# Reading float32 tiles under a float32r name in the transposes of a fused attention and two feed-forward layers

## The chip, the cores and the metric

The program runs on one core of one Trainium2 chip. The metric is the device time of one execution in microseconds, the median of several runs. The profile is one execution of the same program, taken by the hardware profiler.

## The reference

The input is four batches of eight heads, 576 positions and 64 elements a head, all in float32. What is computed is an attention with a threshold, and behind it two feed-forward layers on the 2304 x 512 result:

```
scores = scale * q @ k.T
scores = where(scores >= max(scores) - tau, scores, -1e9)
attn   = exp(scores - max(scores)); attn /= sum(attn) + 1e-9
x = (attn @ v), heads side by side            # 2304 x 512
x = (s * relu(x @ w_in)**2 + b) @ w_out       # 512 -> 2048 -> 512
out = leaky(x @ w2_in) @ w2_out               # the same sizes, one slope for each of 2048 columns
```

## The kernel before

Work is added as tasks (`add`), each with an engine, a planned cost in microseconds, a rank, and the buffers that it reads and writes. `Plan.run` then plays these tasks through on planned costs and writes each engine's instruction order, so that the order of every queue follows from the planned costs as well as from the ranks. The chip afterwards runs each queue in that order.

Attention works on 16 pairs of heads, four pairs to a batch. For a pair, the natural rows of k, q and v are loaded (three `nat` tiles for all pairs, four `v32` tiles of their own for the first four pairs). TensorE (PE) turns k and q in `transpose` at L658 to L662: runs of four transposes of 128 x 128 each (two runs a pair) and one single transpose of the tails. Nine score tiles of 128 x 576 follow (L742). VectorE (DVE) takes the maximum (L752), ScalarE (ACT) the exponentials into one of six `e` tiles (L756), and DVE applies the threshold and sums (L758). `group` then turns five column blocks of the exponentials for each of four groups of a pair, at L874 to L881. Such a run is two transposes at L877 (`gi` is 0), or two at L877 and a third at L881 (`gi` is 1), so there are 160 runs of two and 160 runs of three. ACT, DVE and POOL split each turned block into a high and a low float32r part, and PE multiplies by v at L852. At the end `by_sums` spreads the reciprocals into `rb`, turns them at L811 (12 runs of four, 8 runs of two), and DVE multiplies `z` by them (L814). The result goes to the DRAM tensor `xs`.

All transposes read float32: the tile that is turned is the stationary operand of PE and the identity in `eyes` streams through. The other products outside the first four pairs are float32r with high and low parts (`mm3`, L480 to L482, three passes).

The first feed-forward layer is in two blocks of work. Block A (six blocks of 256 positions, ten of the sixteen slices of the hidden size) has rank `LATER`, so that PE takes it where no attention task is ready. It needs `xs` of its positions. Block B (the rest, 384 positions at a time) may start only when attention has given its memory back and its own rows have been loaded into `xr` (L493) and split into `xb` (L497, L498); ACT and DVE meanwhile turn the remaining weights into float32r halves in `wb` (the last step at L411). The second layer follows with a seven-product scheme.

Of the kernel before, what the change touches and what calls it, by code (L numbers as in the profile page):

```python
# [9 lines left out]
F32 = mybir.dt.float32  # L10
F32R = mybir.dt.float32r
# [6 lines left out]
P = 128  # L18
# [42 lines left out]
class Slots:  # L61
# [4 lines left out]
    def add(self, tiles):  # L66
        self.free.extend(tiles)
# [152 lines left out]
def tile_kernel(ctx: ExitStack, tc: tile.TileContext, q, k, v, tau, w1i, w1o, s_in, b_in, w2i, w2o, alpha, out):  # L220
    nc = tc.nc
    B, H, S, D = q.shape
# [6 lines left out]
    NQ = S // P  # L229
    TL = S - NQ * P  # L230
    NK = NQ + 1
# [9 lines left out]
    add = plan.add  # L241


    def pe(n, k=1):
        return k * max(0.109, n / 2400.0 + 0.0025)

    def pe_r(n, k=1):

        return k * (n / 2400.0 + (0.0135 if n < 512 else 0.0205))
# [17 lines left out]
    const = ctx.enter_context(tc.tile_pool(name="const", bufs=1))  # L267
# [6 lines left out]
    def tiles(pool, n, name, shape, dt=F32):  # L274
        return [pool.tile(shape, dt, name=f"{name}{i}") for i in range(n)]

    eyes = const.tile([P, P + P // 2], F32, name="eyes")
    ident = eyes[:, :P]
    swap = eyes[:, P // 2:]
    tau_b = const.tile([P, 1], F32, name="tau_b")  # L280
    s_b = const.tile([P, 1], F32, name="s_b")
    b_b = const.tile([P, 1], F32, name="b_b")
# [36 lines left out]
    rb_s, yb_s = Slots(), Slots()  # L319

    xt = mp.tile([P, NC * 2 * TA], F32R, name="xt")
    gt = mp.tile([P, NGA * 4 * TA], F32R, name="gt")
# [234 lines left out]

    def attention(ap):
        STEP = 10.0
        nat_s = Slots(tiles(ap, 3, "nat", [P, NK, 2, D]))  # L560
        vt_s, gh_s, gl_s, gr_s = Slots(), Slots(), Slots(), Slots()

        q_s = Slots(tiles(ap, 1, "q", [P, 2, NQ * P], F32R))
        k_s = Slots(tiles(ap, 1, "k", [P, S], F32R))
        hq = ap.tile([P, 2, NK * P], F32R, name="hq")
        hq_s, hk_s = Slots([hq]), Slots(tiles(ap, 1, "hk", [P, 2, S], F32R))
        e_s = Slots(tiles(ap, 6, "e", [P, S]))
        used = []
        used_s, used_v = [[] for _ in range(NP)], [[] for _ in range(NP)]
        gf = tiles(ap, 2, "gf", [P, G2])  # L570
# [3 lines left out]
        for t in gf + sh:  # L574
            nc.gpsimd.memset(t, 0.0)
        z_s = Slots(tiles(ap, 2, "z", [P, S]))
        rb_s = Slots(tiles(ap, 1, "rb", [P, NQ * P]))
        mx_s = Slots(tiles(ap, 4, "mx", [P, 2]))
        sums_s = Slots(tiles(ap, 2, "sums", [P, NS]))
        rc_s = Slots(tiles(ap, 2, "rc", [P, NS]))  # L580
# [24 lines left out]
        def pair(p):  # L605
            whole = p < NP
# [8 lines left out]
            nat = {}  # L615
# [30 lines left out]
            for nm in "kq":  # L646
                t, hl = nat[nm], (ks if nm == "k" else qs)[0] if first else Buf(hk_s if nm == "k" else hq_s)
                qk[nm] = hl
                for tail in (False, True):
                    n, c0 = (TL, NQ * P) if tail else (NQ * P, 0)  # L650
                    c = slice(c0, c0 + n)
                    s0 = TL if tail and nm == "q" else 0
                    if s0:
                        tr = of_tails
                    else:
                        tr = Buf(one_s, {"k": "misc", "q": "gt"}[nm]) if p == 0 and not tail else Buf(moe_s) if whole else Buf(one_s, "misc")

                        def transpose(t=t, tr=tr, cs=(NQ,) if tail else tuple(range(NQ))):  # L658
                            for i, c in enumerate(cs):
                                nc.tensor.transpose(tr.t[:, i * P:(i + 1) * P], t.t[:, c].rearrange("p h d -> p (h d)"), ident)  # L660

                        add("PE", pe(P, 1 if tail else NQ), transpose, (t,), (tr, hl), rank=ready)  # L662
                        if tail:
                            of_tails = tr
                    cut_of = slice(s0, s0 + n)
                    if first:
                        if nm == "k":
                            add("ACT", act(n), lambda hl=hl, tr=tr, c=c, n=n: nc.scalar.activation(
                                k32[p][:, c], tr.t[:, :n], AF.Copy), (tr,), (hl,), rank=ready)
                            continue  # L670
                        for h in range(2):
                            c0 = 2 * NQ * P + h * TL if tail else h * NQ * P

                            def scaled(e, h=h, c=slice(c0, c0 + n), tr=tr, of=cut_of):
                                if e == "DVE":
                                    nc.vector.tensor_scalar(q32[p][:, c], tr.t[:, of], sc_h[h], None, op0=ALU.mult)
                                else:
                                    nc.scalar.activation(q32[p][:, c], tr.t[:, of], AF.Copy, scale=sc_h[h])

                            add([("DVE", dve(n) + 0.065, ready), ("ACT", act(n, 1), ready)], 0, scaled, (tr,), (hl,))  # L680
                        continue
                    if nm == "k":
                        x = add("ACT", act(n), lambda hl=hl, tr=tr, c=c, n=n: nc.scalar.activation(
                            hl.t[:, 0, c], tr.t[:, :n], AF.Copy), (tr,), (hl,), rank=ready)
                        add("DVE", dve(n), lambda hl=hl, tr=tr, c=c, n=n: nc.vector.tensor_tensor(
                            hl.t[:, 1, c], tr.t[:, :n], f32(hl.t[:, 0, c]), op=ALU.subtract), (tr,), (hl,), after=(x,), rank=ready)
                        continue
                    for m, c in ends if tail else ((sc_p, c),):
                        x = add("ACT", act(n, 1), lambda hl=hl, tr=tr, m=m, c=c, of=cut_of: nc.scalar.activation(
                            hl.t[:, 0, c], tr.t[:, of], AF.Copy, scale=m), (tr,), (hl,), rank=ready)  # L690
                        add("DVE", dve(n) + 0.065, lambda hl=hl, tr=tr, m=m, c=c, of=cut_of: nc.vector.scalar_tensor_tensor(
                            hl.t[:, 1, c], tr.t[:, of], m, f32(hl.t[:, 0, c]), op0=ALU.mult, op1=ALU.subtract),
                            (tr,), (hl,), after=(x,), rank=ready)
                for h in () if first else (1, 0):
                    a = half(h)[0]
                    if nm == "k":
                        for i in range(2):
                            hwdge(lambda hl=hl, x=ks[h], a=a, i=i: nc.sync.dma_start(
                                f32(x.t[half(i)[0]]), f32(hl.t[a, i, :])), (hl,), (ks[h],), ready, 147 + BUSY)
                        continue  # L700
                    for i in range(2):
                        hwdge(lambda hl=hl, x=qs[h], a=a, i=i: nc.sync.dma_start(
                            f32(x.t[half(i)[0]]), f32(hl.t[a, :, :NQ * P])), (hl,), (qs[h],), ready, 262 + BUSY)
# [90 lines left out]
        def by_sums(sums, rc, i0, i2, z, rank):  # L794

            pm, rb, c = Buf(one_s, "misc"), Buf(rb_s), slice(i0 * P, i2 * P)

            def tiles_of(t):
                return t.t[:, :2 * NQ].rearrange("p (h i) -> p h i", h=2)

            inverse(sums, rc, lambda t: tiles_of(t)[:, :, i0:i2], rank)

            m = i2 - i0
            add([("POOL", pool1(m * P), rank), ("ACT", act(m * P, 0, True), rank + 1.0)], 0, lambda e: (
                nc.gpsimd.tensor_copy if e == "POOL" else nc.scalar.copy)(
                rb.t[:, :m * P].rearrange("p (i h d) -> p i h d", i=m, h=2),
                tiles_of(rc)[:, :, i0:i2].rearrange("p h i -> p i h").unsqueeze(3).to_broadcast([P, m, 2, D])), (rc,), (rb,))

            def spread():
                for i in range(m):  # L810
                    nc.tensor.transpose(pm.t[:, i * P:(i + 1) * P], rb.t[:, i * P:(i + 1) * P], ident)  # L811

            add("PE", pe(P, m), spread, (rb,), (pm,), rank=rank)
            add("DVE", dve(m * P), lambda: nc.vector.tensor_tensor(z.t[:, c], z.t[:, c], pm.t[:, :m * P], op=ALU.mult),  # L814
                (z, pm), (z,), rank=rank)

# [21 lines left out]
        def group(h, gi, rank, es, vt, via, plain):  # L838
# [26 lines left out]
            for c, before in steps:  # L865
# [6 lines left out]
                keys = slice(S - rows, S) if c == NQ else slice(c * P, (c + 1) * P)  # L872

                def transpose(gt=gt, keys=keys, rows=rows):  # L874
                    m = 0
                    for i in whole:
                        nc.tensor.transpose(gt.t[:rows, m:m + P], es[i].t[:, keys], ident)  # L877
                        m += P
                    if gi:

                        nc.tensor.transpose(gt.t[:rows, m:m + P], es[NQ].t[:, keys], swap if h else ident)  # L881

                add("PE", pe(P, 2 + gi), transpose, [es[i] for i in whole] + ([es[NQ]] if gi else []), (gt,),
                    after=() if plain else ahead(), rank=rank)
                if plain:
                    f = Buf(gp_s if c % 2 else gf_s)
# [68 lines left out]
    with tc.manual_schedule():  # L955
        make_identity(nc, ident)
        nc.vector.tensor_copy(eyes[:, P:], ident[:, :P // 2])
        nc.sync.dma_start(tau_b, tau.unsqueeze(0).to_broadcast([P, 1]))
        nc.vector.tensor_scalar(keep, tau_b, 0.0, None, op0=ALU.is_ge)
        nc.vector.tensor_scalar(sc_p, keep, scale, None, op0=ALU.mult)  # L960
# [363 lines left out]
```

## Time and profile before

| | us |
|---|---|
| median of 3 runs | 1116.73 |
| lowest to highest run | 1116.6 to 1117.04 |
| span of the profiled execution | 1111.8 |
| PE busy in the span | 1090.6 |
| DVE busy | 911.6 |
| ACT busy | 755.5 |

The span runs from the first to the last instruction of the program. The profiled execution has no time of its own beside its span; the median is 4.9 us above the span, and that much lies around the instructions. PE's busy time counts from the start of a matmul to its modelled end. Since matmuls overlap, the distance from one start to the next is shorter than the duration, and two engines' times, PE's and that of its weight loads (PEld), run side by side.

### The profile page before, as it was taken

What the parts mean: (1) busy time and instruction counts of PE and PEld (TensorE: products, weight loads), DVE (VectorE), ACT (ScalarE), POOL (GpSimd) and SP (SyncE); (2) the same over time, 40 slices, a digit from 0 to 9 for tenths busy, and PEclk for the clock granted to TensorE, in tenths of its full rate; (3) what the DMA queues carried; (4) which work ended last, traced back from release to release, by engine and by line L of the source; (5) the groups of instructions that cost most, each with busy time, mean ns of one, the idle gap of its engine ahead of it and who ended that gap; (6) DMA issues with size and microseconds to landing.
All of it is one profiled execution on the core that took longest, in us unless ns stands there. A gap on an engine that the chain in (4) does not pass through costs nothing.

```text
span 1111.8 us, 22073 instructions
## 1 busy us (share of the span) xinstructions
PE 1090.6 (98%) x7536; PEld 1051.7 (95%) x7536; DVE 911.6 (82%) x2055; ACT 755.5 (68%) x1737; POOL 352.1 (32%) x476
## 2 busy tenths in 40 slices
PE   8999999999999999999999999999999999999998
PEld 7777899998999999999999999999999999999998
DVE  4898888879888988757877789589986999998882
ACT  4888878867877868744554377357786998565551
POOL 1576764644654646500000013020120332112111
PEclk9999999999999999999999999999999999999999
DMA  5663363446444454044466565428834464554531
GB/s 119 177 167 123 107 168 86 109 118 156 109 118 118 118 124 108 12 139 134 125 217 209 173 205 161 126 86 278 279 132 164 146 211 154 159 160 119 154 90 39
DMA packets 185265, 158.36 MB, mean 142 GB/s; under 512 B 72000, under 2 KB 162112, under 8 KB 185152
## 3 DMA queue, kind: packets, MB, share of 16 engines
q1 hardware_dynamic: 182624, 154.79, 48.6%
q10 hardware_dynamic: 2528, 2.16, 0.7%
q8 instruction: 59, 0.97, 0.3%
q14 instruction: 54, 0.44, 0.1%
HBM read 91.10 MB, written 44.56 MB: 122 GB/s over the span
## 4 chain that ended last, share of the span: by engine, by line
PE 79%; DVE 9%; ACT 5%; DMA 3%; issue 2%; SPq 1%; POOL 0%; DVEq 0%; ACTq 0%; POOLq 0%
PE bank L480 12%; PE bank L481 11%; PE bank L482 11%; PE bank_b L481 8%; PE bank_b L480 8%; PE bank_b L482 8%; PE bank L852 7%; PE sc L742 7%; PE bank L877 5%; ACT e L756 1%; PE bank L881 1%; DVE e L758 1%; PE bank L660 1%; DMA stg<-wfi 1%; DVE mx L752 1%
## 5 line engine op out<-in xcount | busy, mean ns | idle before, releaser
L758 DVE SCALAR_TENSOR_TENSOR e<-sc,mx,e 128x576 f32<-128x576 f32 x144 | 116.3, 813 | 16.8 <-ACT e L756 13.2
L756 ACT ACTIVATE e<-sc,mx 128x576 f32<-128x576 f32 x144 | 106.4, 742 | 21.4 <-DVE mx L752 20.7
L877 PE MATMUL bank<-eyes,e 128*128 128x128 f32 (+1 forms) x640 | 120.2, 274 | 0.6 <-ACT gf L896 0.3
L752 DVE TENSOR_REDUCE mx<-sc 128x1 f32<-128x576 f32 x144 | 107.0, 751 | 13.7 <-PE sc L742 12.8
L877 PEld LDWEIGHTS bank<-eyes,e 128*128 128x128 f32 (+1 forms) x640 | 80.2, 139 | 13.4 <-issue 1.3
L480 PE MATMUL bank<-xt,wa 128*128 128x256 f32 (+1 forms) x266 | 84.3, 317 | 1.9 <-ACT rest L518 1.1
L480 PE MATMUL bank<-gt,wa 128*128 128x256 f32 (+1 forms) x267 | 83.5, 313 | 0.9 <-ACT rest L518 0.7
L481 PE MATMUL bank<-gt,wa 128*128 128x256 f32 (+1 forms) x267 | 78.9, 295 | 0.2 <-DVE gt L458 0.2
L482 PE MATMUL bank<-gt,wa 128*128 128x256 f32 (+1 forms) x267 | 78.9, 295 | 0.0
L754 POOL TENSOR_SCALAR mx<-mx,tau_s 128x1 f32<-128x1 f32 x144 | 51.4, 358 | 83.7 <-DVE mx L752 80.2
L482 PE MATMUL bank<-xt,wa 128*128 128x256 f32 (+1 forms) x266 | 76.8, 289 | 0.0
L481 PE MATMUL bank<-xt,wa 128*128 128x256 f32 (+1 forms) x266 | 76.7, 289 | 0.0
L742 PE MATMUL sc<-k,q 128*128 128x288 f32 x272 | 65.5, 369 | 1.8 <-DVE e L758 0.9
L852 PE MATMUL bank<-gl,vt 128*128 128x256 f32 (+1 forms) x192 | 64.8, 338 | 1.2 <-POOL gl L907 0.6
L852 PE MATMUL bank<-gh,vt 128*128 128x256 f32 (+1 forms) x192 | 57.8, 301 | 0.1
L541 ACT ACTIVATE gt<-rest,b_b,s_b 128x384 fp32r<-128x384 f32 x56 | 39.5, 708 | 26.5 <-DVE rest L539 26.3
L481 PE MATMUL bank_b<-gt,wa 128*128 128x384 f32 (+1 forms) x168 | 54.4, 324 | 1.1 <-DVE gt L531 1.0
L912 DVE TENSOR_TENSOR gl<-bank,gh 128x256 fp32r<-128x256 f32 (+1 forms) x96 | 43.4, 452 | 14.3 <-ACT gh L910 12.8
L480 PE MATMUL bank_b<-gt,wa 128*128 128x384 f32 (+1 forms) x168 | 54.3, 323 | 0.2 <-ACT n L1174 0.2
L480 PEld LDWEIGHTS bank<-xt,wa 128*128 128x128 f32 x266 | 50.4, 189 | 4.1 <-ACT rest L518 2.2
L482 PE MATMUL bank_b<-gt,wa 128*128 128x384 f32 (+1 forms) x168 | 54.1, 322 | 0.0
L922 POOL TENSOR_TENSOR gr<-gf,gh 64x256 fp32r<-64x256 f32 (+1 forms) x48 | 39.7, 828 | 44.2 <-DVE gl L920 43.0
(649 smaller groups left out, 4158.2 us busy)
## 6 DMA issues: line engine op xcount, KB each, us to landing
stg<-in_moe_w_in_dram SPq DMA_DIRECT2D x32, 512.0 KB, 4.0
stg<-in_moe_w_out_dram SPq DMA_DIRECT2D x32, 512.0 KB, 3.7
qo<-hq SPq DMA_DIRECT2D x32, 256.0 KB, 4.3
gf<-rest SPq DMA_DIRECT2D x30, 192.0 KB, 2.3
rest<-gf SPq DMA_DIRECT2D x40, 128.0 KB, 2.9
ko<-hk SPq DMA_DIRECT2D x32, 144.0 KB, 2.7
xr<-xs SPq DMA_DIRECT2D x6, 768.0 KB, 5.2
yf<-yb SPq DMA_DIRECT2D x24, 192.0 KB, 2.6
```

Of the source, the lines that this page charges most:

```text
L480: nc.tensor.matmul(o, lhsT=wl, rhs=mh, start=first, stop=False, skip_group_check=on_top)
L481: nc.tensor.matmul(o, lhsT=wh, rhs=ml, start=False, stop=False, skip_group_check=on_top)
L482: nc.tensor.matmul(o, lhsT=wh, rhs=mh, start=False, stop=last, skip_group_check=on_top)
L742: nc.tensor.matmul(sp.t[:, x, :HS], lhsT=o[0][:, c], rhs=o[1][:, x * HS:(x + 1) * HS], start=n == 0, stop=n == len(passes) - 1)
L752: add("DVE", dve(S), lambda sp=sp, mx=mx: nc.vector.tensor_reduce(mx.t[:, 0:1], sp.t[:, :, :HS], op=ALU.max, axis=AX.XY, negate=True), (sp ...
L754: t2 = add("POOL", 0.26, lambda mx=mx: nc.gpsimd.tensor_scalar(mx.t[:, 1:2], mx.t[:, 0:1], -1.0, tau_s, op0=ALU.mult, op1=ALU.subtract), ( ...
L756: add("ACT", act(S, 1), lambda sp=sp, mx=mx, e=e: nc.scalar.activation(halves(e.t), sp.t[:, :, :HS], AF.Exp, bias=mx.t[:, 0:1]), (sp, mx), ...
L758: add("DVE", dve(S) + 0.065, lambda sp=sp, mx=mx, e=e, col=col, sums=sums: nc.vector.scalar_tensor_tensor(halves(e.t), sp.t[:, :, :HS], mx ...
L852: nc.tensor.matmul(o.t[:, :n], lhsT=w.rearrange("p a b -> p (a b)"), rhs=m.t[:, :n], start=c == first and x == 0, stop=c == last and x == ...
L877: nc.tensor.transpose(gt.t[:rows, m:m + P], es[i].t[:, keys], ident)
L912: add("DVE", dve(n), lambda hi=hi, lo=lo, gt=gt: nc.vector.tensor_tensor(lo.t[:, :n], gt.t[:, :n], f32(hi.t[:, :n]), op=ALU.subtract), (gt ...
L922: add("POOL", pool2(n), lambda hi=hi, f=f, hf=hf: nc.gpsimd.tensor_tensor(hi.t[:TL, :n], f.t[:TL, :n], f32(hf.t[:TL, :n]), op=ALU.subtract ...
```

## The change

`nat`, `e` and `rb` no longer come from a pool. Each lies at a place counted down from the end of the memory and has two names there, one float32 and one float32r, over the same bytes. A second identity, `eyes_r`, is made in float32r by one copy of 128 x 192 on DVE. In each run of transposes all but the last read the float32r name with the float32r identity and write the bank as float32r; the last one reads float32 as before. The tile `v32` and the writers and other readers of the tiles keep their float32 names. The planner's cost of a run goes from 0.109 us a transpose to `turned(k)`.

```diff
+    def turned(k):
+        return 0.109 + (0.06 + 0.085 * (k - 2) if k > 1 else 0.0)
...
+    def words(name, shape, at):
+        a, r = (nc.alloc_sbuf_tensor_at(name + k, shape, dt, offset=at).ap() for k, dt in (("", F32), ("r", F32R)))
+        as_r[id(a)] = r
+        return a
+
+    as_r, end = {}, [nc.sbuf_usable_end // 32 * 32]
+
+    def placed(n, name, shape):
+        size = 4
+        for k in shape[1:]:
+            size *= k
+        end[0] -= n * size
+        return [words(f"{name}{i}", shape, end[0] + i * size) for i in range(n)]
+
+    def flip(to, x, part, i, n, one, one_r):
+        if i < n - 1:
+            nc.tensor.transpose(to.bitcast(F32R), part(as_r[id(x)]), one_r)
+        else:
+            nc.tensor.transpose(to, part(x), one)
...
+    eyes_r = const.tile([P, P + P // 2], F32R, name="eyes_r")
+    ident_r, swap_r = eyes_r[:, :P], eyes_r[:, P // 2:]
...
-        nat_s = Slots(tiles(ap, 3, "nat", [P, NK, 2, D]))
+        nat_s = Slots(placed(3, "nat", [P, NK, 2, D]))
...
-        e_s = Slots(tiles(ap, 6, "e", [P, S]))
+        e_s = Slots(placed(6, "e", [P, S]))
...
-        rb_s = Slots(tiles(ap, 1, "rb", [P, NQ * P]))
+        rb_s = Slots(placed(1, "rb", [P, NQ * P]))
...
-                                nc.tensor.transpose(tr.t[:, i * P:(i + 1) * P], t.t[:, c].rearrange("p h d -> p (h d)"), ident)
-
-                        add("PE", pe(P, 1 if tail else NQ), transpose, (t,), (tr, hl), rank=ready)
+                                flip(tr.t[:, i * P:(i + 1) * P], t.t, lambda x: x[:, c].rearrange("p h d -> p (h d)"), i, len(cs), ident, ident_r)
+
+                        add("PE", turned(1 if tail else NQ), transpose, (t,), (tr, hl), rank=ready)
...
-                    nc.tensor.transpose(pm.t[:, i * P:(i + 1) * P], rb.t[:, i * P:(i + 1) * P], ident)
-
-            add("PE", pe(P, m), spread, (rb,), (pm,), rank=rank)
+                    flip(pm.t[:, i * P:(i + 1) * P], rb.t, lambda x: x[:, i * P:(i + 1) * P], i, m, ident, ident_r)
+
+            add("PE", turned(m), spread, (rb,), (pm,), rank=rank)
...
+                    of = [(es[i].t, ident, ident_r) for i in whole]
                     if gi:
-
-                        nc.tensor.transpose(gt.t[:rows, m:m + P], es[NQ].t[:, keys], swap if h else ident)
-
-                add("PE", pe(P, 2 + gi), transpose, [es[i] for i in whole] + ([es[NQ]] if gi else []), (gt,),
+                        of.append((es[NQ].t, swap, swap_r) if h else (es[NQ].t, ident, ident_r))
+                    for m, (e, *ones) in enumerate(of):
+                        flip(gt.t[:rows, m * P:(m + 1) * P], e, lambda t: t[:, keys], m, len(of), *ones)
+
+                add("PE", turned(2 + gi), transpose, [es[i] for i in whole] + ([es[NQ]] if gi else []), (gt,),
...
+        nc.vector.tensor_copy(eyes_r, eyes)
```

## Rows read from the trace of the kernel before

**Rows 1.** The page: span, and busy time of PE.

```profile
span 1111.8 us, 22073 instructions
...
PE 1090.6 (98%) x7536; PEld 1051.7 (95%) x7536; DVE 911.6 (82%) x2055; ACT 755.5 (68%) x1737; POOL 352.1 (32%) x476
```

**Rows 2.** Busy time of each engine by stretch: start:end, length, engines, clock, DMA.

```profile
0.00:80.00 80.00, 74.63 (x378) 58.37 (x379) 57.98 (x133) 56.66 (x131) 37.84 (x64) 1.00 0.63 157
80.00:120.00 40.00, 39.96 (x227) 31.86 (x227) 35.15 (x74) 33.51 (x71) 27.71 (x30) 1.00 0.40 125
120.00:480.00 360.00, 352.12 (x2813) 341.41 (x2812) 305.08 (x714) 277.36 (x629) 200.77 (x292) 1.00 0.44 109
480.00:514.00 34.00, 32.30 (x263) 31.58 (x262) 22.82 (x42) 12.96 (x24) 0.00 (x0) 1.00 0.55 174
```

**Rows 3.** The same for instructions on the tile eyes alone: PE, PEld, DVE, POOL.

```profile
0.00:80.00 80.00, 32.96 (x189) 26.52 (x189) 0.21 (x1) 0.50 (x2) 1.00 0.63 157
80.00:120.00 40.00, 12.31 (x80) 9.81 (x81) 0.00 (x0) 0.00 (x0) 1.00 0.40 125
120.00:480.00 360.00, 128.67 (x773) 92.53 (x772) 0.00 (x0) 0.00 (x0) 1.00 0.44 109
```

**Rows 4.** Groups by shape on PE: count, then busy us, mean ns, idle before.

```profile
L877 PE MATMUL bank<-eyes,e 128*128 128x128 f32 x608 | 114.3, 274 | 0.6 <-ACT gf L896 0.3
...
L482 PE MATMUL bank<-gt,wa 128*128 128x256 f32 x200 | 56.5, 282 | 0.0
...
L480 PE MATMUL bank_b<-gt,wa 128*128 128x384 f32 x128 | 42.9, 335 | 0.2 <-ACT n L1174 0.2
...
L742 PE MATMUL sc<-ko,qo 128*128 128x288 f32 x256 | 45.1, 303 | 2.6 <-DVE e L758 1.9 <-DMA qo<-hq 0.7
```

**Rows 5.** Timeline of PE around two runs of transposes: start us, us.

```profile
201.69 0.28 PE L482 MATMUL bank<-xt,wa 128*128 128x256 f32 x1
201.81 0.39 PE L877 MATMUL bank<-eyes,e 128*128 128x128 f32 x2
202.04 0.27 PE L881 MATMUL bank<-eyes,e 128*128 128x128 f32 x1
...
203.01 0.38 PE L877 MATMUL bank<-eyes,e 128*128 128x128 f32 x2
203.23 0.27 PE L881 MATMUL bank<-eyes,e 128*128 128x128 f32 x1
```

**Rows 6.** Timeline of the weight loads in the same stretch.

```profile
201.76 0.20 PEld L877 LDWEIGHTS bank<-eyes,e 128*128 128x128 f32 x2
201.93 0.14 PEld L881 LDWEIGHTS bank<-eyes,e 128*128 128x128 f32 x1
202.04 0.19 PEld L480 LDWEIGHTS bank<-xt,wa 128*128 128x128 f32 x1
202.15 0.19 PEld L481 LDWEIGHTS bank<-xt,wa 128*128 128x128 f32 x1
```

**Rows 7.** Groups by shape of the weight loads.

```profile
L877 PEld LDWEIGHTS bank<-eyes,e 128*128 128x128 f32 x608 | 76.7, 140 | 10.6 <-DVE e L758 0.8 <-ACT gf L896 0.7 <-DVE gl L920 0.7
L481 PEld LDWEIGHTS bank<-gt,wa 128*128 128x128 f32 x267 | 50.6, 190 | 0.5 <-DVE gt L458 0.5
```

**Rows 8.** Timeline of the SP queue: a late load for block A, and attention's end.

```profile
388.57 1.13 SPq L493 DMA_DIRECT2D stg<-xs  x1
...
480.23 0.32 SPq L788 DMA_DIRECT2D xs<-z  x1
...
483.82 0.37 SPq L493 DMA_DIRECT2D xr<-xs  x1
```

**Rows 9.** Timeline of DVE: the start, block B's rows, the last weights.

```profile
1.33 0.21 DVE L957 COPY eyes<-eyes 128x64 f32<-128x64 f32 x1 [1.33 <-POOL by_half L961]
3.48 0.15 DVE L959 TENSOR_SCALAR keep<-tau_b 128x1 f32<-128x1 f32 x1 [1.93 <-DMA tau_b<-in_tau_dram]
...
495.59 0.55 DVE L498 TENSOR_TENSOR xb<-xr,xb 128x384 fp32r<-128x384 f32 x1
...
549.83 0.69 DVE L411 TENSOR_TENSOR wb<-n,wb 128x512 fp32r<-128x512 f32 x1
```

**Rows 10.** Timeline of PE: block B's first product, and the first on new weights.

```profile
513.74 0.34 PE L480 MATMUL bank_b<-xb,wa 128*128 128x384 f32 x1
...
551.18 0.33 PE L480 MATMUL bank<-xb,wb 128*128 128x384 f32 x1
```

More of the change, by code (lines that the diff above doesn't have):

```diff
@@ L874, in transpose @@
                 def transpose(gt=gt, keys=keys, rows=rows):
[L875 to L878, printed above, removed]
+                    of = [(es[i].t, ident, ident_r) for i in whole]
                     if gi:
-                        nc.tensor.transpose(gt.t[:rows, m:m + P], es[NQ].t[:, keys], swap if h else ident)
-                add("PE", pe(P, 2 + gi), transpose, [es[i] for i in whole] + ([es[NQ]] if gi else []), (gt,),
+                        of.append((es[NQ].t, swap, swap_r) if h else (es[NQ].t, ident, ident_r))
+                    for m, (e, *ones) in enumerate(of):
+                        flip(gt.t[:rows, m * P:(m + 1) * P], e, lambda t: t[:, keys], m, len(of), *ones)
+                add("PE", turned(2 + gi), transpose, [es[i] for i in whole] + ([es[NQ]] if gi else []), (gt,),
                     after=() if plain else ahead(), rank=rank)
```

## The prediction

> **What bounds the kernel now.** I read the page first: of a span of 1111.8 us PE is busy 1090.6 [rows 1]. That is a share of modelled durations, so the next view is the busy time by stretch. Up to 80 us PE is idle for over 5 us of 80. From 80 to 120 us it is busy 39.96 of 40, from 120 to 480 us 352.1 of 360, while DVE, the next engine, has 35.2 and 305.1, and the granted clock is 1.00 throughout, its 2.4 GHz level [rows 2]. So PE sets the pace from 80 us on, with DVE 85 to 88% full right behind it.
>
> What PE does there is attention first and block A in the holes. Whether a hole is worth something depends on whether block A always has work waiting. The SP queue answers that: the last load for block A goes out at 388.6 us, attention's last store at 480.2, and block B's first product starts only at 513.7 [rows 8, 10]. Between 480 and 514 us PE is busy 32.3 of 34 [rows 2], with block A. So there is a backlog of some 30 us of block A when attention ends, and PE time saved inside attention is filled by it.
>
> Next, what a transpose costs. Those on `eyes` are 773 between 120 and 480 us, 80 between 80 and 120, and 189 before 80, of which 32 are warm-up products and not transposes [rows 3]. A transpose's start follows the one before after 0.11 us (203.01 to 203.23 for two) [rows 5]; its mean duration is 274 ns [rows 4], so about 164 ns of it is a tail that overlaps with the next. A float32r product of 256 columns gives way after 0.12 us (201.69 to 201.81) [rows 5] with 282 ns, a tail of 162, and one of 384 columns has 335 [rows 4]. The tails agree, so differences of durations are differences of pace. 128 more float32r columns cost 53 ns, which is one column a tick at 2.4 GHz, and 128 float32 columns take twice that.
>
> **The change part by part.** Of k transposes in a run k-1 become float32r. 160 runs of two give 160, 160 runs of three give 320, and the 32 runs of four on `nat`, 12 of four and 8 of two on `rb` give 96 + 36 + 8 = 140. Together 620 change, out of 800 + 144 + 64 = 1008; 372 of them (one in each run) stand right ahead of a float32 transpose, 248 ahead of another float32r one.
>
> *The streaming.* A float32r transpose has no row here, nor has any float32r product under 256 columns. Carried down from the two shapes it would last 282 - 53 = 229 ns, 45 less than 274 [rows 4], so follow at 0.065 instead of 0.11 us. That is the most I count. The least is nothing, because the next weight load may take its place.
>
> *The weight load ahead of a float32 transpose.* At 201.76 us such a load starts and its transpose starts at 201.81 [rows 5, 6], so it needs about 50 ns and fits under 65. The 372 save 45 ns each: 16.7 us.
>
> *The weight load ahead of a float32r transpose.* The plain float32r load is recorded with 190 ns against 140 [rows 7], 50 more, so about 100 instead of 50 to fill the array; two of them in a row start 0.11 apart [rows 6]. If a float32r transpose loads like that, the 248 save about nothing; if it loads like a float32 transpose, 45 each, 11.2 us. Nothing lies nearer to either end, and I take the middle, 5.6 us.
>
> The Trainium skill, "TensorE: Matmul & The Clock Gate", section "LDWEIGHTS (loading the stationary operand)", gives the load a time of its column count over 1.2 GHz, whatever the type. By it every load here takes 107 ns, no transpose can follow faster than now, and the sum would be 0 instead of 22.3. The 0.05 us from load to start in the float32 transpose speaks against it, the 0.11 us between float32r loads for it.
>
> *The first load of a run* becomes float32r too. It starts under a product of 0.12 us or more, so even 100 ns hide but for some 5 ns; with 372 runs that is at most 1.9 us, and I count 1. The last transpose and the float32r load behind it are as before.
>
> *At the start* DVE makes `eyes_r`. Its copy of 64 columns took 0.21 us, and DVE then idles 1.93 us for the load of tau [rows 9]. A copy of 192 columns, three times that at most, fits into this hole; without it, it would cost its 0.6 us once. Places instead of pool tiles add no instruction and no DMA, and the waits for `e`, `nat` and `rb` have the same writers.
>
> *The sum.* 16.7 + 5.6 - 1 = 21.3 us of PE time. 853 of the 1008 transposes lie behind 80 us, where PE is full: 85%, 18.0 us. Of the 3.3 us ahead of 80 us PE idles anyway for a part; I count half, 1.6. That makes 19.6 us.
>
> *What is late next.* Block A would then end near 494 us. Block B needs its rows: loaded from 483.8 us, last split at 495.6 + 0.55 = 496.1 [rows 8, 9]. If attention's end stays at 480 us, block B's start can move from 513.7 to 496.1 at most, 17.6 us; if attention ends earlier, this moves too. The last remaining weights are done at 550.5 us, and the first product on new weights is at 551.2 [rows 9, 10]; those on the last unit come four slices later, near 568, since a slice of block B takes 4.2 us (513.7 to 551.2 holds ten first products and, lagging by two, eight second ones, and a slice is one of each). So the weights allow about 17 us as well. DVE, 85% full, will not let attention shorten by the whole 20 us. I take 17 us: span 1094.8, and with the 4.9 us around it 1099.7, call it 1100 us.
>
> **The rivals.** The forecast case is 1091 to 1108 us: the lower price has the 248 save nothing (16.7 - 1.9 = 14.8 us, 85% and half the rest 13.7, less 3 for a stall at block B's start: 1106), the upper one has all 620 save 45 ns (27.9 us, 25.8 reach the end if attention ends earlier too: 1091). Chance 0.66.
>
> *More than that*, with a float32r transpose at one column a tick and no fixed part (53 ns instead of 109, 620 x 56 = 34.7 us): 1085 to 1091 us. Attention would have to end 15 us earlier, against which DVE's 85% speaks. Chance 0.05.
>
> *The load sets the pace.* Every weight load fills for 0.11 us, in a transpose too, and all 620 follow as now: no change, 1115 to 1118 us. The two float32r loads 0.11 us apart speak for it, the 0.05 us from load to start of a float32 transpose against it [rows 5, 6]. It is the rule of the Trainium skill's section named above. Chance 0.06. *Given back at the end.* Attention ends some 17 us later, because block A's work on DVE and ACT comes sooner and pushes attention's back, and block B waits for its rows by as much as was saved: 1114.5 to 1119 us. DVE's 85% leaves room for the same work [rows 2], which speaks against it. Chance 0.04. *A small part* reaches it (the order of the queues changes everywhere with the planner's 24.2 us less on PE, 168 x 0.049 + 160 x 0.073 + 44 x 0.097, and DVE waits grow): 1108 to 1114.5. Chance 0.08.
>
> *Slower.* The longer load is not hidden: inside a run the transpose has only 65 ns of streaming to hide a load of 100 and its start-up, recorded as 50 ns longer [rows 7]. If the load comes wholly behind the product ahead of it, the pace is 65 + 100 ns = 0.165 instead of 0.11, 55 ns more for each of the 620 (34.1 us, of which 85% and half the rest arrive, 31.5: 1148 us). It decides from the point where a float32r transpose follows later than 0.11 us. Against it: in float32 the second load starts 0.06 us after the first (two take 0.20 us, one 0.14 [rows 6]), at 201.82, with the first one's product still to stream. Chance 0.11.
>
> **How the numbers follow.** A change under 0.2% (2.2 us) could not be told from none. Faster is 0.66 + 0.05 + 0.08 = 0.79, the same 0.10, slower 0.11. The range leaves out the slow case and the most extreme gain: 1090 to 1118. The likeliest case alone is 1091 to 1108.
>
> **What would show it.** In the profile of the changed kernel, starts inside a run of two should be 0.065 us apart, in runs of three 0.065 to 0.11 for the first step; durations of float32r transposes near 230 ns; their weight loads between 140 and 190 ns. Block B's first product should start near 496 us, attention's last store between 465 and 480, and the stretch behind 560 us should keep its length. The prediction is wrong if the pace stays at 0.11, if DVE's waits let PE run empty before 480 us, or if PE waits for `xb` or `wb` for more than 5 us behind attention.

## The result and the profile after

The changed kernel runs in 1106.54 us (median of 4 runs, 1105.83 to 1108.07), the kernel before in 1116.66 beside it. The ratio is 0.9918, with a 95% interval of 0.9904 to 0.9932: 9.2 us faster, 7.6 to 10.7. That lies inside the range of 1090 to 1118, on the side that was forecast, and the gain is about 0.55 of the 17 us.

The page of the changed kernel first (span, busy time, the chain that ended last by engine):

```profile
span 1104.0 us, 22088 instructions
...
PE 1072.1 (97%) x7536; PEld 1032.0 (93%) x7536; DVE 924.6 (84%) x2076; ACT 749.3 (68%) x1727; POOL 341.5 (31%) x466
...
PE 75%; DVE 11%; ACT 5%; DMA 4%; issue 2%; SPq 1%; POOL 0%; DVEq 0%; ACTq 0%
```

The span is 7.8 us shorter than in [rows 1]. This profiled execution took 1105.83 us, 1.8 us more than its span, and every later run lies 1.7 to 2.3 us above its span, those of the kernel before included (1115.41 us with a span of 1113.6). So the 4.9 us of the prediction were not time around the instructions: if the same 1.8 us lie around the profiled execution of before, it was some 3 us quicker than the median run.

Busy time by stretch (start:end, length, PE, PEld, DVE, ACT, POOL, clock, DMA), to hold beside [rows 2]:

```profile
0.00:80.00 80.00, 70.04 (x373) 54.94 (x374) 59.19 (x130) 57.09 (x128) 31.79 (x57) 0.96 0.55 142
80.00:120.00 40.00, 37.80 (x223) 29.57 (x222) 37.59 (x84) 32.48 (x71) 24.07 (x29) 1.00 0.53 153
120.00:480.00 360.00, 348.78 (x2884) 334.75 (x2882) 315.67 (x722) 276.96 (x629) 203.22 (x293) 1.00 0.45 110
480.00:514.00 34.00, 31.99 (x239) 31.34 (x240) 24.02 (x42) 15.13 (x30) 1.04 (x2) 1.00 0.54 175
```

PE has lost busy time in every stretch of attention, and from 120 to 480 us it got through only 71 products more (2884 against 2813). Had the 17 us that 773 of the 1008 transposes save (of 22.7, below) been filled with products 0.12 us apart, it would have been some 145. The granted clock of 0.96 ahead of 80 us is a short piece at the 1.2 GHz level, between about 9 and 15 us, behind a stretch in which PE was busy for 0.78 of 2 us:

```profile
6.00:8.00 2.00, 0.78 (x6) 0.61 (x6) 0.75 (x1) 0.00 (x0) 0.00 (x0) 1.00 0.56 125
...
10.00:12.00 2.00, 2.00 (x5) 1.43 (x6) 0.00 (x0) 0.20 (x1) 0.00 (x0) 0.50 0.88 200
```

The kernel before has 1.56 us of PE in the same 2 us, and 1.00 throughout. Of the eight kernels here and below whose first transposes read float32r, five show such a piece ahead of 16 us, and of the six others one does (the kernel before with half its exponentials). It cost next to nothing: the kernel below that has the same order and float32r in every transpose keeps 1.00 here, and is only 0.1 us ahead of the changed kernel at 20 us.

Timeline of PE around a run of two, of three and of four (line numbers are some 25 higher than before; L296 is the float32r transpose, L298 the last one):

```profile
200.50 0.22 PE L296 MATMUL bank<-eyes_r,e4r 128*128 128x128 f32 x1
200.56 0.28 PE L298 MATMUL bank<-eyes,e 128*128 128x128 f32 x1
200.59 0.37 PE L505 MATMUL bank<-xt,wa 128*128 128x256 f32 x1
200.80 0.28 PE L506 MATMUL bank<-xt,wa 128*128 128x256 f32 x1
...
201.03 0.22 PE L296 MATMUL bank<-eyes_r,e5r 128*128 128x128 f32 x1
201.09 0.23 PE L296 MATMUL bank<-eyes_r,e0r 128*128 128x128 f32 x1
201.16 0.30 PE L298 MATMUL bank<-eyes,e 128*128 128x128 f32 x1
...
202.41 0.38 PE L296 MATMUL bank<-eyes_r,nat1r 128*128 128x128 f32 x3
202.62 0.30 PE L298 MATMUL bank<-eyes,nat 128*128 128x128 f32 x1
202.68 0.36 PE L505 MATMUL bank<-xt,wa 128*128 128x256 f32 x1
202.88 0.28 PE L506 MATMUL bank<-xt,wa 128*128 128x256 f32 x1
```

And the weight loads in the same place:

```profile
200.40 0.14 PEld L296 LDWEIGHTS bank<-eyes_r,e4r 128*128 128x128 f32 x1
200.50 0.14 PEld L298 LDWEIGHTS bank<-eyes,e 128*128 128x128 f32 x1
200.56 0.19 PEld L505 LDWEIGHTS bank<-xt,wa 128*128 128x128 f32 x1
...
201.04 0.14 PEld L296 LDWEIGHTS bank<-eyes_r,e0r 128*128 128x128 f32 x1
201.12 0.14 PEld L298 LDWEIGHTS bank<-eyes,e 128*128 128x128 f32 x1
```

The pace is what was hoped for. A float32r transpose lasts 0.22 us and the next starts 0.06 us behind it. The start of the product behind a run is recorded early, so a run is best measured to the second float32r product behind it. From a run's first start to that one, where two products of 256 columns follow, the medians are 0.339, 0.448 and 0.558 us before for runs of two, three and four, and 0.294, 0.379 and 0.466 now (for two: 200.50 to 200.80 above). With 168, 160 and 44 runs that is 168 x 0.045 + 160 x 0.069 + 44 x 0.092 = 22.7 us of PE time.

The ends of the stages, from the SP queue, PE and DVE:

```profile
484.08 0.32 SPq L813 DMA_DIRECT2D xs<-z  x1
...
486.22 0.37 SPq L518 DMA_DIRECT2D xr<-xs  x1
```

```profile
506.59 0.34 PE L505 MATMUL bank<-xb,wa 128*128 128x384 f32 x1
```

```profile
1.57 0.26 DVE L981 CAST eyes_r<-eyes 128x192 fp32r<-128x192 f32 x1
3.48 0.15 DVE L983 TENSOR_SCALAR keep<-tau_b 128x1 f32<-128x1 f32 x1 [1.65 <-DMA tau_b<-in_tau_dram]
```

Attention's last store is 3.9 us later than in [rows 8], block B starts 7.1 us earlier than in [rows 10], and nothing behind that changes length. The copy at the start is hidden. So of 22.7 us of PE time, 7 to 10 reach the end. The question is where the rest went.

### The profile page after: what moved, and what is told of

It is laid out like the page before. It is cut to its first block, busy times and chain, and to the rows that moved or that the text cites. A ratio compares the mean times of both kernels' runs of the same rounds, so it can differ in the third digit from the quotient of the medians.

```text
span 1104.0 us, 22088 instructions
## 1 busy us (share of the span) xinstructions
PE 1072.1 (97%) x7536; PEld 1032.0 (93%) x7536; DVE 924.6 (84%) x2076; ACT 749.3 (68%) x1727; POOL 341.5 (31%) x466
## 4 chain that ended last, share of the span: by engine, by line
PE 75%; DVE 11%; ACT 5%; DMA 4%; issue 2%; SPq 1%; POOL 0%; DVEq 0%; ACTq 0%
PE bank L505 11%; PE bank L506 11%; PE bank L507 11%; PE bank_b L506 8%; PE bank_b L507 8%; PE bank_b L505 8%; PE bank L877 6%; PE sc L767 6%; PE bank L298 3%; PE bank L296 3%; DVE e L783 2%; DVE mx L777 1%; ACT e L781 1%; DMA stg<-xs 1%; SPq L645 1%
## 5 line engine op out<-in xcount | busy, mean ns | idle before, releaser
L777 DVE TENSOR_REDUCE mx<-sc 128x1 f32<-128x576 f32 x144 | 106.8, 750 | 11.4 <-PE sc L767 10.6
L505 PE MATMUL bank<-gt,wa 128*128 128x256 f32 (+1 forms) x367 | 115.7, 315 | 0.5 <-ACT xr L1198 0.4
L506 PE MATMUL bank<-gt,wa 128*128 128x256 f32 (+1 forms) x367 | 110.3, 300 | 0.3 <-DVE gt L556 0.3
L507 PE MATMUL bank<-gt,wa 128*128 128x256 f32 (+1 forms) x367 | 110.3, 300 | 0.0
L298 PE MATMUL bank<-eyes,e 128*128 128x128 f32 (+1 forms) x320 | 90.3, 288 | 2.0 <-DVE e L783 1.9
L505 PE MATMUL bank<-xt,wa 128*128 128x256 f32 (+1 forms) x262 | 81.4, 311 | 3.8 <-ACT rest L543 3.2
L506 PE MATMUL bank<-xt,wa 128*128 128x256 f32 (+1 forms) x262 | 75.1, 287 | 0.0
L507 PE MATMUL bank<-xt,wa 128*128 128x256 f32 (+1 forms) x262 | 75.0, 286 | 0.0
L779 POOL TENSOR_SCALAR mx<-mx,tau_s 128x1 f32<-128x1 f32 x144 | 47.5, 331 | 81.8 <-DVE mx L777 78.3
L505 PEld LDWEIGHTS bank<-gt,wa 128*128 128x128 f32 x367 | 70.4, 192 | 1.2 <-ACT xr L1198 0.7
L506 PEld LDWEIGHTS bank<-gt,wa 128*128 128x128 f32 x367 | 69.5, 189 | 0.5 <-DVE gt L556 0.5
L507 PEld LDWEIGHTS bank<-gt,wa 128*128 128x128 f32 x367 | 69.4, 189 | 0.0
L767 PEld LDWEIGHTS sc<-k,q 128*128 128x128 f32 x272 | 44.9, 195 | 10.3 <-DVE e L783 3.8
L563 ACT ACTIVATE rest<-bank_b 128x384 f32<-128x384 f32 x39 | 19.1, 490 | 50.7 <-PE bank_b L507 50.6
```

What stands on the lines that cost most here:

```text
L298: nc.tensor.transpose(to, part(x), one)
L505: nc.tensor.matmul(o, lhsT=wl, rhs=mh, start=first, stop=False, skip_group_check=on_top)
L506: nc.tensor.matmul(o, lhsT=wh, rhs=ml, start=False, stop=False, skip_group_check=on_top)
L507: nc.tensor.matmul(o, lhsT=wh, rhs=mh, start=False, stop=last, skip_group_check=on_top)
L767: nc.tensor.matmul(sp.t[:, x, :HS], lhsT=o[0][:, c], rhs=o[1][:, x * HS:(x + 1) * HS], start=n == 0, stop=n == len(passes) - 1)
L777: add("DVE", dve(S), lambda sp=sp, mx=mx: nc.vector.tensor_reduce(mx.t[:, 0:1], sp.t[:, :, :HS], op=ALU.max, axis=AX.XY, negate=True), (sp ...
```

## The experiments

**Order and speed apart.** The change does two things: it makes transposes faster, and it tells the planner so, which changes the order of every queue. Two kernels separate them.

```diff
     def turned(k):
-        return 0.109 + (0.06 + 0.085 * (k - 2) if k > 1 else 0.0)
+        return pe(P, k)
```

> The change with the planner's old cost of 0.109 us a transpose: every queue has the order of the kernel before (one copy more on DVE), and 620 transposes read float32r. Theory A, PE time saved before block A's third block has its rows (about 256 us) turns into idle time of PE, whatever the order: 1104 to 1109 us, as the changed kernel. Theory B, the new order of the queues cost most of the saving: 1096 to 1101 us, 16 to 20 us under the kernel before, and attention's last store at 478 us or earlier.

Measured: 1106.57 us, ratio 0.9915 (0.9899 to 0.9931). The time is that of theory A, and the old order does not give the saving back: theory B falls. The other sign of theory B did come, attention's last store at 478 us or earlier:

```profile
472.67 0.32 SPq L813 DMA_DIRECT2D xs<-z  x1
```

So attention's end alone does not tell the time.

```diff
     def flip(to, x, part, i, n, one, one_r):
-        if i < n - 1:
-            nc.tensor.transpose(to.bitcast(F32R), part(as_r[id(x)]), one_r)
-        else:
-            nc.tensor.transpose(to, part(x), one)
+        nc.tensor.transpose(to, part(x), one)
```

> The changed kernel's order of the queues with every transpose reading float32. Theory A, the order is worth little: 1115 to 1119 us. Theory B, the new order costs about 8 us: 1122 to 1128 us.

Measured: 1121.42 us, ratio 1.0047 (1.0031 to 1.0063). That is between the two expectations: the order that was planned for fast transposes costs 5 us when they are slow, and nothing, against the old order, when they are fast (0.9918 and 0.9915). In the new order the transposes pay 14.4 us by the quotient of the two ratios (uncertain by some 2 us), in the old one 9.5. The last store of attention comes late in this order:

```profile
499.18 0.32 SPq L810 DMA_DIRECT2D xs<-z  x1
```

With fast transposes it came at 484.08 us. So the speed moved it forward by 15.1 us in the new order and by 7.6 in the old one (480.23 to 472.67); that the changed kernel ends attention later than the kernel before is the work of the order.

**Early and late apart.** In the order of before, float32r in one half of the pairs:

```diff
-    def flip(to, x, part, i, n, one, one_r):
-        if i < n - 1:
+    def flip(to, x, part, i, n, one, one_r, fast):
+        if fast and i < n - 1:
...
-                        flip(gt.t[:rows, m * P:(m + 1) * P], e, lambda t: t[:, keys], m, len(of), *ones)
+                        flip(gt.t[:rows, m * P:(m + 1) * P], e, lambda t: t[:, keys], m, len(of), *ones, rank < 72 * STEP)
```

(Pairs 0 to 7 have these ranks; `>=` takes pairs 8 to 15. The runs on `nat` and `rb` go the same way.)

> The order of the kernel before, float32r in the transposes of the first eight pairs alone (308 of 620, about 11 us of PE time). Theory A, PE has no other work to put into the time saved there: 0 to 3 us faster than before, 1113.5 to 1117. Theory B, the saving is used wherever it arises: 1106 to 1109 us.

> The order of the kernel before, float32r in the transposes of the last eight pairs alone (312 of 620, about 11 us of PE time). Theory A, nearly all of it arrives, since block A has work in hand there: 1105 to 1108 us. Theory B, the same as for the first eight pairs: 1106 to 1109 us.

Measured: 1111.93 us for the early half, ratio 0.9963 (0.9949 to 0.9977), and 1111.58 for the late one, 0.9957 (0.9941 to 0.9973). Both halves pay, 4.1 and 4.8 us of about 11 each; together that is 8.9 us beside the 9.5 of all, the same within their uncertainty of some 1.6 us each. Theory A falls as well: the saving is not lost where block A has no work in hand; some 0.4 of it arrives in either half. Theory B is right that the halves are alike, but with 1106 to 1109 us it missed the size in both. Since the queues of these kernels hold the same products in the same order, the start of each PE instruction can be set against its start in the other kernel. Microseconds earlier, at the time given:

```
at us                                        80   160   240   320   400   480   560  1080
all float32r, old order, against before    -0.7   0.5   2.2   3.6   5.3   7.6   7.6   7.2
early half, against before                  0.0   1.5   3.1   2.1   2.1   2.5   2.5   1.9
late half, against before                  -1.4  -1.4  -1.6  -1.6   0.1   2.2   2.2   1.9
changed kernel, against its order in f32    1.1   3.8   6.1   8.8  11.6  14.4  15.1  15.6
```

The kernel with all 620 gains nothing in the first 80 us, and from there to attention's end about 2 us in every 80. In the halves the growth is less even: the late half, whose fast transposes begin at 231 us, gains nothing up to 320, and the early half gives back 1 us after its last one at 243. Each row is one execution against one: the late half is 1.4 us behind at 80 us, where no transpose of it is fast, so that much lies between two executions. With this caution, no single place behind 80 us loses the saving.

The distances between the ends of neighbouring PE products, all float32r against before up to 515 us, sum up to the -7.6 us like this (a change of up to 0.06 us in one distance is called pace, a larger one a wait):

```
pace                                       -17.9
waits longer:  product by v                 +4.9
               transpose                    +4.4
               score                        +3.3
               block A                      +0.5
waits shorter                               -2.8
sum                                         -7.6
```

So the rest is handed back in waits of PE, ahead of products by v (which need the split on ACT, DVE and POOL), of transposes (which need exponentials or a free bank) and of scores (which need DVE to free one of two score tiles). Of the 13.1 us of longer waits 5.4 lie ahead of 80 us, and there PE's idle time shows them: its busy time falls from 74.63 us [rows 2] to 69.55. The other 7.6 us lie behind 80 us, at 52 products. At 37 of these, with 4.1 us, PE has no idle time on record, since the wait ends within the modelled duration of the product ahead. PE's busy time fell only from 352.1 us [rows 2] to 349.15 in 360:

```profile
0.00:80.00 80.00, 69.55 (x375) 53.32 (x376) 57.35 (x131) 55.89 (x128) 37.13 (x62) 0.98 0.62 153
...
120.00:480.00 360.00, 349.15 (x2868) 334.63 (x2867) 303.74 (x714) 277.79 (x631) 200.29 (x292) 1.00 0.45 113
```

**Is it DVE, ACT, or the chain through both?** Work was taken from one engine, with slow and with fast transposes, every other instruction and the order left alone:

```diff
-    mx.t[:, 0:1], sp.t[:, :, :HS], op=ALU.max, axis=AX.XY, negate=True), ...
+    mx.t[:, 0:1], sp.t[:, 0:1, :HS], op=ALU.max, axis=AX.XY, negate=True), ...
```

```diff
-    halves(e.t), sp.t[:, :, :HS], AF.Exp, bias=mx.t[:, 0:1]), ...
+    halves(e.t)[:, 0:1], sp.t[:, 0:1, :HS], AF.Exp, bias=mx.t[:, 0:1]), ...
```

> The kernel before, with the maximum of each score tile taken over its first 288 columns alone (a part of the computation is left out): some 0.3 us less on DVE in each of 144 tiles, 43 us in all, every queue in the same order. Theory C, DVE is as near to the bound as PE: a gain of its own of 3 to 10 us. Theory D, ACT is what PE waits for: under 3 us.

> The same cut in the maximum together with the float32r transposes in the order of the kernel before. Theory C: the transposes now pay more than the 9 us that they pay beside the full maximum, 13 to 18 us against the other kernel with half the maximum. Theory D and theory F (the way from a transpose through the split to the product is itself the limit): 8 to 10 us again.

> The kernel before, with the exponentials taken over the first 288 columns alone (a part of the computation is left out, the tiles are set to zero once on POOL at the start): some 0.24 us less on ACT in each of 144 tiles, 35 us in all. Theory C: under 3 us of gain, apart from DVE's waits for the exponentials. Theory D: 3 to 10 us.

> Half the exponentials together with the float32r transposes in the order of the kernel before. Theory D: the transposes pay 13 to 18 us against the other kernel with half the exponentials. Theories C and F: 8 to 10 us.

> The kernel before with half the maximum and half the exponentials (both cuts of the runs before together; part of the computation is left out). PE's work is unchanged and PE is what bounds this kernel: 2 to 5 us faster than before, 1110 to 1113.

> The same two cuts together with the float32r transposes in the order of the kernel before. Theory G, the rest of the saving is lost in waits for the chain maximum, exponentials, threshold, on DVE and ACT: the transposes pay 16 to 21 us against the other kernel with both cuts, 1091 to 1096. Theory F, the waits arise behind the transposes (evacuation, split, product) and not in this chain: 12 to 14 us, as with one cut alone, 1098 to 1100.

| cut | float32 transposes, ratio | float32r, ratio | what float32r pays |
|---|---|---|---|
| none | 1 | 0.9915 (0.9899 to 0.9931) | 9.5 us |
| half the maximum (DVE) | 0.9984 (0.9972 to 0.9996) | 0.9873 (0.9858 to 0.9887) | 12.4 us |
| half the exponentials (ACT) | 0.9990 (0.9980 to 1.0000) | 0.9871 (0.9854 to 0.9887) | 13.3 us |
| both | 0.9947 (0.9928 to 0.9965) | 0.9845 (0.9827 to 0.9862) | 11.4 us |

(The last column is one minus the quotient of the two ratios, times 1116 us; by their intervals it is uncertain by some 2 to 3 us.) The cuts took 38 us from DVE (911.6 to 874.0 us busy) and 30 us from ACT (755.5 to 725.9). With slow transposes either is worth 1 to 2 us: PE bounds that kernel, as the prediction read it. With float32r transposes they are worth about 5 us each. This points to DVE and ACT having moved closer to the bound, which was the point of theories C and D, but each cut raises the pay by only 3 to 4 us, hardly outside the uncertainty, and neither engine alone is the bound.

No theory came out whole. Theory C missed its 13 to 18 us with 12.4, and its own gain of 3 to 10 us with 1.8; theory D reached 13.3 us, but with 1.1 us instead of 3 to 10 beside slow transposes; theory F missed its 8 to 10 us with both. Both cuts together gave 1109.47 us beside slow transposes, 5.9 us less than before where 2 to 5 were expected, and 1098.24 us beside float32r ones. What the transposes pay does not rise further by that; theory G, with 16 to 21 us, falls. The time of 1098.24 us lies in theory F's range of 1098 to 1100, its pay of 11.4 us just under 12 to 14. Half of the saving stays out even with the maximum and the exponentials halved (the threshold on DVE stayed whole). That speaks for theory F, that the waits arise behind the transposes, but no run relieved that way, so it is not shown. Which of the remaining hand-offs (evacuation, split, free bank) holds most of it was not settled.

**The last transpose.** The changed kernel with the last one of each run float32r as well:

```diff
-        if i < n - 1:
-            nc.tensor.transpose(to.bitcast(F32R), part(as_r[id(x)]), one_r)
-        else:
-            nc.tensor.transpose(to, part(x), one)
+        nc.tensor.transpose(to.bitcast(F32R), part(as_r[id(x)]), one_r)
```

> The changed kernel with the last transpose of each run float32r too, in the same order of every queue. Theory H, the last one is hidden anyway because the plain float32r weight load behind it needs its 0.11 us, and its own load then takes 0.085 instead of 0.06 to start: 0.02 us more for each of 372 runs, 0 to 6 us slower than the changed kernel, 1106 to 1112. Rival: the last one follows faster as well, 372 times 0.045 us less on PE, of which four tenths arrive: 1098 to 1101 us.

Measured: 1114.32 us, ratio 0.9984 (0.9973 to 0.9996), so 0.9984 / 0.9918 = 1.0067 of the changed kernel, 7.4 us slower. This is theory H in its direction and in its 0.02 us a run (below), and a little over its bound of 6 us, which was set too low for its own 372 x 0.02 = 7.4. A run of two in its timeline:

```profile
201.72 0.22 PE L295 MATMUL bank<-eyes_r,e4r 128*128 128x128 f32 x1
201.79 0.22 PE L295 MATMUL bank<-eyes_r,e3r 128*128 128x128 f32 x1
201.84 0.35 PE L502 MATMUL bank<-xt,wa 128*128 128x256 f32 x1
202.03 0.28 PE L503 MATMUL bank<-xt,wa 128*128 128x256 f32 x1
```

```profile
201.73 0.14 PEld L295 LDWEIGHTS bank<-eyes_r,e3r 128*128 128x128 f32 x1
201.81 0.19 PEld L502 LDWEIGHTS bank<-xt,wa 128*128 128x128 f32 x1
201.92 0.19 PEld L503 LDWEIGHTS bank<-xt,wa 128*128 128x128 f32 x1
```

From the first start to the second product it is 0.31 us instead of 0.30 above; the medians are 0.313, 0.399 and 0.486 us against 0.294, 0.379 and 0.466, 0.02 more in each of 372 runs. The weight load of the product behind starts 0.08 us after the last transpose's load instead of 0.06 (200.50 to 200.56 above), and needs its 0.11 us until the next. By the medians the added PE time arrives whole, while of the 22.7 us taken away 14.4 arrived. The two traces bear this out only in part: product by product, this kernel is 3.5 us behind the changed one when attention ends, and a further 2.2 us arise behind 560 us, where no transpose runs. Its twelve runs also spread from 1111.1 to 1117.0 us, and the seven with a mean granted clock of 0.996 or less are 2 us longer on average than the five with more. So that added time arrives whole is not shown.

**Another order.** One constant of the changed kernel, the rank of the early output weights:

```diff
-W1O = 200, 15
+W1O = 300, 15
```

> The changed kernel with another order of the queues: the early output weights get rank 300 instead of 200, so that their work on DVE and ACT comes later. If waits on DVE and ACT eat the saving, an order with less of their work early may give back some of it: 1098 to 1106 us. If the order is worth nothing: 1105 to 1109.

Measured: 1100.20 us, ratio 0.9860 (0.9847 to 0.9874), 15.6 us under the kernel before and some 6 under the changed one. It is the fastest kernel here that leaves nothing out. Attention ends later still, at 488.0 us, yet block B starts 5.9 us earlier than in the changed kernel:

```profile
488.03 0.33 SPq L813 DMA_DIRECT2D xs<-z  x1
...
490.19 0.37 SPq L518 DMA_DIRECT2D xr<-xs  x1
```

```profile
500.65 0.34 PE L505 MATMUL bank<-xb,wa 128*128 128x384 f32 x1
```

So another order is worth some 6 us here, where the faster transposes are worth 9.5 in the old order. That this order wins because the weights' work on DVE and ACT comes later was only argued; one order against another shows no more than that orders differ by this much.

## Why the prediction was right and where it was off

*What bounds the kernel* was read rightly: PE. With slow transposes, 38 us less work on DVE or 30 on ACT are worth 1 to 2 us.

*The streaming and the weight loads* came out nearly as worked out. Ahead of a float32 transpose the pace is 0.06 us where 0.065 was carried down from wider products; the float32r duration of 229 ns was 0.22 to 0.23 us. The open term, the 248 ahead of another float32r transpose, was put in the middle between nothing and 45 ns each; runs of three save 24 ns more than runs of two (69 against 45), so the middle of 22 ns was right. The loads of float32r transposes are recorded with 0.14 us as the float32 ones, not with 0.19. In all 22.7 us against 22.3, or 21.3 with the 1 us for the first load. The rival in which the load sets the pace is answered by these rows: transposes follow at 0.06 us, where it had 0.11. The section of the Trainium skill that stands beside it ("TensorE: Matmul & The Clock Gate", "LDWEIGHTS (loading the stationary operand)") gives a load of 128 columns 107 ns; the trace does not agree for transposes, whose next load starts 0.06 to 0.09 us later.

*The share that arrives* is the term that was mis-sized: "853 of the 1008 transposes lie behind 80 us, where PE is full: 85%". With half of the rest, the sum let 19.6 of 21.3 us arrive, 0.92 of them. Measured in the old order it is 9.5 of 22.7, about 0.4. The step took PE's busy time, 352.1 us of 360, for proof that nothing else ends PE's waits there. But each product carries some 160 ns of tail, and a wait shorter than that leaves no idle time on record. With PE faster, results of DVE, ACT and POOL come last more often, and PE hands back some 10 us in waits (13.1 longer, 2.8 shorter). Ahead of 80 us, where half was counted, nothing arrived in that order. The new order, which the sum put at nothing, is worth a second look: with slow transposes it costs 5.2 us, and with the 14.4 us that the speed pays there this makes the 9.2 us of the change. The backlog of block A was real and did not help: the chip runs each queue in the planned order, so block A fills a wait only where the plan has put it there. Why results come late, and through which engine, stays open.

*What is late next* was wrong in its place. Block B's start was forecast near 496 us with attention's end between 465 and 480; they came at 506.6 and 484.1, and the late end of attention comes from the new order (499.2 us with slow transposes). The cap of 17.6 us at block B's start was never reached. The rival in which a small part reaches the end (1108 to 1114.5, chance 0.08) names the mechanism that acted, growing waits and a changed order, and the forecast's own case holds the size. That is in part luck: the slow bound of this case, 1106 us, was worked out with the 248 saving nothing and a stall of 3 us at block B's start. Neither happened, and the measured time lies at this bound by the waits instead.

*The 4.9 us around the span* were 1.8. With 1.8 the predicted span of 1094.8 us would have given 1096.6 us instead of 1099.7, so this error hid 3 us of the other one. Measured by spans the gain is 7.8 us, by medians 10.

*The copy at the start* went as foreseen: it took 0.26 us inside the wait for tau.

## What to carry to other kernels

A PE that is busy 98% in the profile may still be waiting in pieces shorter than its products' tails, so work taken from it arrives only as far as the other engines' results can come sooner: here to four tenths in one order and six tenths in another. Where a list of instructions is planned ahead, the chip here kept to the plan, and a backlog did not fill the new holes; plan again with the new costs, and try more than one plan, since two orders of the changed kernel differed by 6 us. To tell speed from order, run the new speed in the old order and the old speed in the new one. In a run of transposes, the last one is best left float32 where a float32r weight load follows: this saved 0.02 us a run here.

## What the runs showed of the hardware that was not expected

The recorded weight load of a transpose is short in both types, 0.14 us against 0.19 for a plain float32r load. What separates the types is the start of the next load: in runs of two it comes 0.06 us behind the load of a float32 transpose (200.50 to 200.56) and 0.08 behind that of a float32r one (201.04 to 201.12 in a run of three, 201.73 to 201.81). This fits what the runs pay: a step of 0.085 us instead of 0.109 is the 24 ns by which a second float32r transpose shortens a run, where the one ahead of the float32 transpose saves 45. It fits the end of a run as well: from the load of the last transpose to that of the second product behind it the median is 0.173 us where the last one is float32, and 0.194 where it is float32r, in runs of two and of three alike.
